# A spectral mixing kernel rewritten: row axis folded twice, products summed by matmul on 32x32 tiles, units of four PSUM banks

## The chip, the cores and the metric

The kernel runs on one core of a Trainium2 chip. The metric is the device time of one execution in microseconds. A profile of one execution shows each engine: PE (TensorE matmul; PEld its weight loads), DVE (VectorE), ACT (ScalarE), POOL (GpSimd) and SP, which here only issues transfers.

## The reference

Two inputs `A` and `B` each have spectral weights, both are applied to the same `x` (1 x 2048 x 1024, bf16), and a gate mixes the results:

```python
g = sigmoid((x * gate_w).sum(-1, keepdims=True))
X = rfft2(x.astype(float32))                 # over 2048 rows and 1024 columns
a = irfft2(X * (A_w_r + 1j * A_w_i)).astype(bfloat16)
b = irfft2(X * (B_w_r + 1j * B_w_i)).astype(bfloat16)
return g * a + (1 - g) * b
```

`w_r` and `w_i` are 2048 x 513. The transforms are computed as matmuls with constant cosine and sine matrices; the gate enters in the inverse row transform.

## The kernel before

The row index is split as s = 16 s2 + s1, with 128 values of s2 on the partitions and 16 of s1 along the free axis. The work goes through these steps:

- **f1** (L214 to L228): for each s1, eight matmuls (L218) of 256 columns transform along s2. The halves d and d + 512 are added and subtracted by the same matmuls (constants F and -F), so that frequencies along d fall into even and odd ones. A copy per s1, on ACT or DVE in turn (L226, L228), puts the result into `y`.
- **f2** (`f2`, L275): the transform along d, for one parity and a pair of row groups (a unit, n = 0 to 15: eight of even and then eight of odd columns): eight matmuls of 512 columns into a PSUM tile of two banks; ACT copies it to `T` (L279).
- **f3** (`f3`, L295, L303): the 16-point transform along s1 with twiddles, on 64x64 tiles of the array; for even columns also the extra column at the end of the spectrum, in a PSUM tile `pl` of its own, copied by DVE (L313). ACT copies the main part to `X` (L310).
- **cmul** (L325, L330, L331): on DVE, two products of X's real and imaginary part with the four weight matrices, then a subtraction and an addition that give the complex product `Y`.
- **i1** (L344): the inverse of f3, on 64x64 tiles, real and imaginary part apart; ACT copies each into `rl` (L349), and after the second POOL issues two DMAs (L354) that bring the rows into another order, into `Re` or `Ro`.
- **i2** (L367): the inverse transform along s2, with the gate multiplied into its constants (`EA`, `EB`), for a parity and two values of s1: 16 matmuls of 128 columns; ACT copies to `V` (L370).
- **i3** (L378): the inverse along d, eight matmuls of 512 columns. The even half is kept as fp32 (L384 on ACT, L386 on DVE); for the odd half DVE adds and subtracts (L389, L390), and SP stores the result (L391).
- **the gate**: `gate_hat` (L241) applies the gate's weights in the transformed domain, ACT copies (L245), a DMA from ACT's queue reshapes (L246), and `gate_z` (L254, L256) transforms back and takes the sigmoid. `gate_weights` (L261, L262) makes `EA` and `EB`.

The order of instructions on each engine is written out by hand in the loops from L394: unit n is in f2 while n - 1 is in f3 and cmul and n - 3 is in i1. `gate_hat` follows f2(0), and `gate_z` is issued at n = 2; the even half's i2 and i3 are woven into the last odd units; the rest of i2 and i3 follows alone. PSUM is used as three rotating tiles of two banks (`pp`) and one more tile. Engines work through their own queues in order; semaphores are set by the framework from the tiles that each instruction reads and writes.

Of the kernel before, what the change touches and what calls it, by code (L numbers as in the profile page):

```python
# [10 lines left out]
P = 128  # L11
S = 2048
D = 1024
NT = 16
NU = 8
# [5 lines left out]
WID = (257, 256)  # L21
PIT = (258, 256)
# [6 lines left out]
def quad_reps(t):  # L29
    return (0, 32, 16, 48) if t == 0 else (t, t + 32, t + 64, t + 96)  # L30


def half_k2(t, jh):
    a, b = quad_reps(t)[2 * jh:2 * jh + 2]
    if t == 0 and jh == 0:
        return (0, 64, 32, 96)
    return (a, 128 - a, b, 128 - b)


def half_rows(t, jh):  # L40
    return np.array([k2 + 128 * k1 for k2 in half_k2(t, jh) for k1 in range(16)])


def unit_rows(t):
    h = (0, 1) if t % 2 == 0 else (1, 0)
    return np.concatenate([half_rows(t, jh) for jh in h])


def make_constants():
    c = {}  # L50
    s2 = np.arange(128)
    F = np.zeros((128, NT, 2, 2, 2))
    E = np.zeros((NT, 2, 2, 2, 128))
    EZ = np.zeros((NT, 2, 2, 2, 128))
    for t in range(NT):
        for j, k2 in enumerate(quad_reps(t)):
            th = 2 * np.pi * s2 * k2 / 128
            F[:, t, j // 2, 0, j % 2] = np.cos(th)
            F[:, t, j // 2, 1, j % 2] = -np.sin(th)
            E[t, j // 2, 0, j % 2] = np.cos(th)  # L60
            E[t, j // 2, 1, j % 2] = np.sin(th)
            EZ[t, j // 2, 0, j % 2] = 2 * np.cos(th)
            EZ[t, j // 2, 1, j % 2] = -2 * np.sin(th)
            if k2 == 0:
                F[:, t, j // 2, 1, j % 2] = np.cos(np.pi * s2)
                E[t, j // 2, 1, j % 2] = np.cos(np.pi * s2)
                EZ[t, j // 2, 0, j % 2] = 1
                EZ[t, j // 2, 1, j % 2] = np.cos(np.pi * s2)
    F = F.reshape(128, 128)
    c["F1"] = _bf16np(np.concatenate([F, -F], axis=1))  # L70
    c["E"] = _bf16np(E.reshape(4, 4, 8, 128).transpose(0, 2, 1, 3).reshape(128, 128))
    c["EZ"] = _bf16np(EZ.reshape(128, 128) / 128)
    d1 = np.arange(512)
    i = np.arange(256)
    FD = np.zeros((512, 2, 2, 256))
    IG = np.zeros((2, 2, 256, 512))
    for eo in range(2):
        m = 2 * i + eo
        ph = 2 * np.pi * np.outer(d1, m) / D
        FD[:, eo, 0] = np.cos(ph)  # L80
        IG[eo, 0] = 2 * np.cos(ph).T
        if eo == 0:
            IG[0, 0, 0] = 1
        m = 2 * i + (2 if eo == 0 else 1)
        ph = 2 * np.pi * np.outer(d1, m) / D
        FD[:, eo, 1] = -np.sin(ph)
        IG[eo, 1] = -2 * np.sin(ph).T
        if eo == 0:
            FD[:, 0, 1, 255] = np.cos(np.pi * d1)
            IG[0, 1, 255] = np.cos(np.pi * d1)  # L90
    IG /= S * D
    c["FD"] = _bf16np(FD.reshape(4, 128, 2, 512).transpose(1, 2, 0, 3))
    c["IG"] = _bf16np(IG.reshape(2, 2, 2, 128, 512).transpose(3, 0, 1, 2, 4).reshape(128, 8, 512))
    s1 = np.arange(NS1)
    WF = np.zeros((128, NT, 3, 64))
    WI = np.zeros((128, NT, 3, 64))
    for t in range(NT):
        for jh in range(2):
            k = half_rows(t, jh)
            reps = quad_reps(t)[2 * jh:2 * jh + 2]  # L100
            al = np.zeros((NS1, 2, 2, 64), dtype=complex)
            be = np.zeros((2, 2, NS1, 64), dtype=complex)
            for p in range(64):
                w = np.exp(-2j * np.pi * k[p] * s1 / S)
                kk = k[p] % 128
                if kk in (0, 64):
                    cc = 0 if kk == 0 else 1
                    al[:, cc, 0, p] = w
                    be[cc, 0, :, p] = w.conj()
                    continue  # L110
                eps = 1 if kk in reps else -1
                j = reps.index(kk if eps > 0 else 128 - kk)
                al[:, 0, j, p] = w
                al[:, 1, j, p] = 1j * eps * w
                be[0, j, :, p] = w.conj()
                be[1, j, :, p] = 1j * eps * w.conj()
            al = al.reshape(64, 64)
            be = be.reshape(64, 64).T
            h = slice(64 * jh, 64 * jh + 64)
            WF[h, t, 0], WF[h, t, 1], WF[h, t, 2] = al.real, al.imag, -al.imag  # L120
            h = h if t % 2 == 0 else slice(64 - 64 * jh, 128 - 64 * jh)
            WI[h, t, 0], WI[h, t, 1], WI[h, t, 2] = be.real, be.imag, -be.imag
    c["WF"] = _bf16np(WF)
    c["WI"] = _bf16np(WI)
    return c
# [3 lines left out]
def gated_mix(ctx, tc, x_in, we_in, wo_in, gw_in, out):  # L129
# [5 lines left out]
    w_in = (we_in, wo_in)  # L135

    const = ctx.enter_context(tc.tile_pool(name="const", bufs=1))
    big = ctx.enter_context(tc.tile_pool(name="big", bufs=1))
    wp = ctx.enter_context(tc.tile_pool(name="wp", bufs=1))
    wk = ctx.enter_context(tc.tile_pool(name="wk", bufs=2))  # L140
    pp = ctx.enter_context(tc.tile_pool(name="pp", bufs=3, space=bass.MemoryType.PSUM))
    pl_pool = tc.alloc_tile_pool(name="plp", bufs=1, space=bass.MemoryType.PSUM)
# [4 lines left out]
    def ptile():  # L147
        return pp.tile([P, 1024], F32, name="pt", tag="pt")

    ctx.enter_context(tc.manual_schedule())  # L150
    warm = const.tile([P, 512], BF16, name="warm")
    nc.vector.memset(warm[:], 0.0)
    wps = ptile()
    for _ in range(6):
        nc.tensor.matmul(wps[:, 0:512], lhsT=warm[:, 0:128], rhs=warm[:], start=True, stop=True)  # L155
    F1 = const.tile([P, 2, 128], BF16, name="f1")
    nc.scalar.dma_start(F1[:].rearrange("p a b -> p (a b)"), dr["F1"])
    gws = const.tile([P, 8], BF16, name="gws")
    nc.scalar.dma_start(gws[:], gw_in)
    Re = big.tile([P, 16 * 1024], BF16, name="re")  # L160
    Ro = big.tile([P, 16 * 1024], BF16, name="ro")
    x = Re[:].rearrange("p (s d) -> p s d", s=NS1)
    for s0, n in ((0, 1), (1, 1), (2, 2), (4, 2), (6, 2), (8, 2), (10, 2), (12, 2), (14, 2)):
        nc.sync.dma_start(x[:, s0:s0 + n, :], xv[:, s0:s0 + n, :])
    FD = const.tile([P, 2, 4, 512], BF16, name="fd")
    WF = const.tile([P, NT, 3, 64], BF16, name="wf")
    WI = const.tile([P, NT, 3, 64], BF16, name="wi")
    IG = const.tile([P, 8, 512], BF16, name="ig")
    Ec = const.tile([P, 128], BF16, name="ec")
    Ez = const.tile([P, 128], BF16, name="ez")  # L170

    y = big.tile([P, 4, 2, 2 * NT, NS1, 4], BF16, name="y")
    Ws = {}
    wt = [wp.tile([P, 2064], BF16, name=f"w{k}", tag=f"w{k}") for k in range(4)]

    def load_w(n):
        par, u = n // NU, n % NU
        if n < 4 or 8 <= n < 12:
            w = wt[n % 4][:]
        elif n < 8:  # L180
            w = Ro[:, (n - 4) * 2064:(n - 3) * 2064]
        else:
            w = y[:, n - 12, 0].rearrange("p t s c -> p (t s c)")
        w = w[:, 0:8 * PIT[par]].rearrange("p (t a m) -> p t a m", t=2, a=4)
        nc.sync.dma_start(w, w_in[par][u])
        Ws[n] = w

    nc.sync.dma_start(FD[:, 0], dr["FD"][:, 0])
    nc.sync.dma_start(WF[:, 0:4], dr["WF"][:, 0:4])
    load_w(0)  # L190
    nc.sync.dma_start(Ez[:], dr["EZ"])
    nc.sync.dma_start(WI[:, 0:4], dr["WI"][:, 0:4])
    load_w(1)
    nc.sync.dma_start(WF[:, 4:16], dr["WF"][:, 4:16])
    load_w(2)
    nc.sync.dma_start(WI[:, 4:16], dr["WI"][:, 4:16])
    nc.sync.dma_start(Ec[:], dr["E"])
    for n in range(3, 8):
        load_w(n)
    nc.sync.dma_start(FD[:, 1], dr["FD"][:, 1])  # L200
    nc.sync.dma_start(IG[:], dr["IG"])

    gwz = const.tile([P, 8, 32], BF16, name="gwz")
    nc.gpsimd.memset(gwz[:], 0.0)
    gh = const.tile([P, 8], F32, name="gh")
    junk = const.tile([P, 8], F32, name="junk")
    nc.scalar.activation(junk[:], gwz[:, 0, 0:8], ACT.Sigmoid)
    nc.vector.tensor_scalar(gh[:], gws[:], 0.5, None, ALU.mult)
    gq = gwz[:].rearrange("p (q e) c -> p q e c", e=2)
    nc.vector.tensor_tensor(gq[:, :, 0, 0], gh[:, 0:4], gh[:, 4:8], ALU.add)  # L210
    nc.vector.tensor_tensor(gq[:, :, 1, 0], gh[:, 0:4], gh[:, 4:8], ALU.subtract)
# [54 lines left out]
    def hp(jh):  # L266
        return slice(64 * jh, 64 * jh + 64)
# [219 lines left out]
```

## Time and profile before

| | us |
|---|---|
| median of three runs | 145.82 (144.42 to 145.93) |
| profiled execution: its own time / its span | 144.42 / 144.4 |
| PE busy | 121.9 |
| DVE busy | 97.6 |
| ACT busy | 93.3 |
| POOL busy | 19.6 |

Matmuls count as busy from their start to a modelled end and overlap, so PE's busy time is not its work at full rate. Granted TensorE clock over the execution: 0.961 of full speed. Transfers: 29.19 MB in all, 20.55 MB from SP's queue and 8.41 MB from POOL's.

The page names a group of instructions by line, engine, operation, output and input. In a timeline a row has start, length, engine, line, operation, shapes and count; in square brackets stands what the engine waited for before it.

### The profile page before, as it was taken

To read this page: it belongs to the slowest core of one execution; us is meant where nothing else is said; L and a number is where in the kernel's file an instruction comes from. 1 tells how busy PE (TensorE), PEld (TensorE's weight loads), DVE (VectorE), ACT (ScalarE), POOL (GpSimd) and SP (SyncE) were. 2 spreads that over 40 slices of the span, in tenths; PEclk is the share of its full clock that TensorE was granted. 3 is DMA by queue.
4 is the path that set the end of the run, shared out by engine and by line. 5 is a ranking of instruction groups with operands and counts; after the bars stand their busy time and mean duration, and the time that the engine had idled before them with its cause. 6 is when DMAs were issued, how large, how long until landed. Compare 5 with 4: busy or idle time off the path is not lost.

```text
span 144.4 us, 2878 instructions
## 1 busy us (share of the span) xinstructions
PE 121.9 (84%) x1188; PEld 68.1 (47%) x1206; DVE 97.6 (68%) x113; ACT 93.3 (65%) x97; POOL 19.6 (14%) x37
## 2 busy tenths in 40 slices
PE   6999979929899898888867999868869999999910
PEld 2688844416344443334324345433455665756500
DVE  0177740089279999999999279599433456898990
ACT  4255546665699999999995899997935244253200
POOL 1000000000033222233333033033330000000000
PEclk9999999975799999999999999999999999999985
DMA  4999999968716999999865315527464000464553
GB/s 148 298 361 419 406 411 405 415 244 284 297 14 168 240 279 278 353 250 202 163 139 133 126 18 140 131 43 168 110 166 110 0 0 0 167 253 166 208 228 145
DMA packets 11088, 29.19 MB, mean 202 GB/s; under 512 B 3781, under 2 KB 4165, under 8 KB 10949
## 3 DMA queue, kind: packets, MB, share of 16 engines
q1 hardware_dynamic: 6048, 20.55, 38.3%
q0 software_dynamic: 4608, 8.41, 24.8%
q8 instruction: 9, 0.15, 0.5%
q10 hardware_dynamic: 420, 0.07, 0.3%
q14 instruction: 3, 0.02, 0.0%
HBM read 16.42 MB, written 4.19 MB: 143 GB/s over the span
## 4 chain that ended last, share of the span: by engine, by line
PE 55%; ACT 24%; DMA 9%; issue 4%; DVE 2%; another core or an unknown queue 2%; DVEq 1%; POOL 0%; ACTq 0%; POOLq 0%
PE pt L378 18%; PE pt L218 10%; PE pt L275 10%; ACT rl L349 10%; PE pv L367 9%; DMA re<-rl 5%; DMA zt<-zs 4%; ACT X L310 4%; ACT T L279 3%; PE pt L344 3%; ACT V L370 2%; PE pt L155 2%; ACT zs L245 2%; DVE ot L390 2%
## 5 line engine op out<-in xcount | busy, mean ns | idle before, releaser
L275 PE MATMUL pt<-fd,y 128*128 128x512 bf16 x117 | 30.5, 394 | 3.8 <-ACT rl L349 2.6
L349 ACT CAST rl<-pt 128x1024 bf16<-128x1024 f32 x32 | 32.9, 1038 | 0.0
L378 PE MATMUL pt<-ig,V 128*128 128x512 bf16 x121 | 29.6, 379 | 1.1 <-ACT V L370 0.7
L370 ACT CAST V<-pv 128x1024 bf16<-128x1024 f32 x16 | 16.3, 1021 | 19.2 <-PE pv L367 19.2
L344 PE MATMUL pt<-Y,wi 64*64 64x512 bf16 x256 | 20.1, 387 | 3.8 <-ACT T L279 0.8
L275 PEld LDWEIGHTS <-y 128*128 128x128 bf16 x128 | 12.6, 100 | 20.3 <-issue 8.6
L279 ACT CAST T<-pt 128x1024 bf16<-128x1024 f32 x16 | 16.3, 1017 | 8.3 <-PE pt L275 4.1
L378 PEld LDWEIGHTS <-V 128*128 128x128 bf16 x128 | 11.7, 98 | 13.9 <-ACT V L370 1.9
L354 POOL DMA_DIRECT2D re<-rl x16 | 9.6, 606 | 59.8 <-ACT rl L349 59.8
L310 ACT CAST X<-pt 128x1024 bf16<-128x1024 f32 x16 | 16.5, 1033 | 0.0
L218 PE MATMUL pt<-f_84,re 128*128 128x256 bf16 x128 | 15.6, 289 | 0.0
L218 PEld LDWEIGHTS <-re 128*128 128x128 bf16 x128 | 13.0, 103 | 3.1 <-DMA re<-in_x_dram 0.8
L228 ACT CAST y<-pt 128x1024 bf16<-128x1024 f32 x8 | 8.1, 1013 | 8.4 <-PE pt L218 8.4
L354 POOL DMA_DIRECT2D ro<-rl x16 | 9.5, 596 | 26.4 <-ACT rl L349 26.4
L386 DVE COPY re<-pt 128x1024 f32<-128x1024 f32 x5 | 6.1, 1225 | 10.2 <-PE pt L378 10.2
L226 DVE CAST y<-pt 128x1024 bf16<-128x1024 f32 x7 | 8.6, 1225 | 5.2 <-PE pt L218 5.2
L344 PEld LDWEIGHTS <-wi 64*64 64x64 bf16 x256 | 6.4, 106 | 11.9 <-issue 10.7
L389 DVE TENSOR_TENSOR ot<-pt,re 128x1024 bf16<-128x1024 f32 x8 | 9.8, 1224 | 3.0 <-PE pt L378 3.0
L367 PE MATMUL pv<-ea,re 128*128 128x128 bf16 x64 | 8.1, 219 | 2.9 <-DMA re<-rl 1.7
L295 PE MATMUL pt<-T,wf 64*64 64x512 bf16 (+2 forms) x192 | 9.8, 307 | 0.4 <-ACT T L279 0.3
L367 PEld LDWEIGHTS <-re 128*128 128x128 bf16 x128 | 7.5, 98 | 5.4 <-issue 2.5
L390 DVE TENSOR_TENSOR ot<-re,pt 128x1024 bf16<-128x1024 f32 x8 | 9.7, 1210 | 0.0
(96 smaller groups left out, 128.2 us busy)
## 6 DMA issues: line engine op xcount, KB each, us to landing
re<-rl POOLq DMA_DIRECT2D x16, 256.0 KB, 8.0
ro<-rl POOLq DMA_DIRECT2D x16, 256.0 KB, 5.1
out_dram<-ot SPq DMA_DIRECT2D x8, 512.0 KB, 2.6
re<-in_x_dram SPq DMA_DIRECT2D x7, 512.0 KB, 8.6
ro<-in_we_dram SPq DMA_DIRECT2D x4, 516.0 KB, 8.0
y<-in_wo_dram SPq DMA_DIRECT2D x4, 512.0 KB, 6.5
fd<-cst_fd SPq DMA_DIRECT2D x2, 512.0 KB, 9.1
ig<-cst_ig SPq DMA_DIRECT2D x1, 1024.0 KB
```

Of the source, the lines that this page charges most:

```text
L218: nc.tensor.matmul(ps[:, q * 256:(q + 1) * 256], lhsT=x[:, s1, h * 512 + q * 128:h * 512 + (q + 1) * 128], rhs=(bc(F1[:, 0, :]).to_broadca ...
L275: nc.tensor.matmul(ps[:, tt * 512:(tt + 1) * 512], lhsT=y[:, q, par, 2 * t:2 * t + 2, :, :].rearrange("p j s c -> p (j s c)"), rhs=FD[:, p ...
L279: nc.scalar.copy(out=T[:].rearrange("p a b -> p (a b)"), in_=ps[:])
L295: nc.tensor.matmul(ps[ho, tt * 512 + dst:tt * 512 + dst + ln], lhsT=WF[hp(jh), 2 * u + tt, w, :], rhs=T[hp(jh), tt, src:src + ln], start=( ...
L310: nc.scalar.copy(out=xo, in_=ps[:].rearrange("p (t r m) -> p t r m", t=2, r=2))
L344: nc.tensor.matmul(ps[hp(jh), tt * 512:(tt + 1) * 512], lhsT=WI[hin, 2 * u + tt, w, :], rhs=Y[hin, k, 2 * tt:2 * tt + 2, o:o + 256], start ...
L349: nc.scalar.copy(out=rl[:, :, r, :], in_=ps[:].rearrange("p (t m) -> p t m", t=2))
L354: nc.gpsimd.dma_start(RR[par][p0:p0 + 29:4, :, :], rl[:, tt].rearrange("p r m -> p (r m)"))
L367: nc.tensor.matmul(ps[:, s * 512 + ch * 128:s * 512 + ch * 128 + 128], lhsT=RR[par][:, s1, c0 + 256 * ab:c0 + 256 * ab + 128], rhs=Ew[:, s ...
L370: nc.scalar.copy(out=V[:].rearrange("p s c k -> p (s c k)"), in_=ps[:])
L378: nc.tensor.matmul(ps[:, s * 512:(s + 1) * 512], lhsT=V[:, s, ch, :], rhs=IG[:, par * 4 + ch, :], start=(ch == 0), stop=(ch == 3))
L390: nc.vector.tensor_tensor(ot[:, :, 1, :], ev, pv, ALU.subtract)
```

## The change

The kernel is rewritten; what is computed stays. The parts:

- **Second fold along d.** Input columns are permuted on the host into the order i, 511 - i, 512 + i, 1023 - i (i = 0 to 255), and the output is permuted back. On the chip `fold` adds and subtracts the halves d and d + 512 with DVE or POOL instructions (for the first s1 `f1u` does it in the matmuls as before), and f1's matmuls add and subtract the mirrored quarters. f2 then contracts 256 values of d in place of 512 for each of cosine and sine.
- **i3 folded likewise.** It makes the cosine and the sine part for 256 values of d apart; `ce` copies both to bf16, `pm` adds and subtracts them (two instructions of 512 elements, DVE or POOL) and `fin` combines the even and the odd half (two of 1024).
- **32x32 tiles.** f3 and i1 work on groups of four row frequencies, 32 partitions by 32, sixteen tiles of the array at a time, over four PSUM banks.
- **No sums on DVE.** `prod` leaves the two products as they are; i1 takes their four terms in four accumulating matmuls per tile, in place of two on `Y`.
- **Units of four banks** (8 units in place of 16), with one PSUM tile of eight banks addressed by bank; copies span one to four banks and are shared between ACT and DVE by a list.
- **Odd columns first**: units 0 and 1 are odd, 2 to 5 mixed, 6 and 7 even; i2 and i3 run over the odd half and then over the even half.
- **The last column of the even spectrum** is computed for all units at once (`pre1`, `pre2`, matmuls of one column) and copied into place by POOL (`xn`).
- **Order**: one list, `ORDER`, gives the sequence of all steps with PSUM bank and engine.

```diff
+UNITS = [[(4 * h + b, 1) for b in range(4)] for h in range(2)]
+UNITS += [[(2 * u, 0), (2 * u, 1), (2 * u + 1, 0), (2 * u + 1, 1)] for u in range(4, 8)]
+UNITS += [[(4 * h + b, 0) for b in range(4)] for h in range(2)]
...
+    def fold(s0, n, eng):
+        e = nc.vector if eng == "d" else nc.gpsimd
+        for k, op in enumerate((ALU.add, ALU.subtract)):
+            e.tensor_tensor(xf[:, s0:s0 + n, 512 * k:512 * k + 512], x[:, s0:s0 + n, 0:512], x[:, s0:s0 + n, 512:1024], op)
...
+    def f1(s1, g0):
+        for uv in range(2):
+            for blk in range(2):
+                for h in range(2):
+                    c0 = uv * 512 + h * 256 + blk * 128
+                    nc.tensor.matmul(PS[:, g0 + uv, blk * 256:blk * 256 + 256], lhsT=xf[:, s1, c0:c0 + 128],
+                                     rhs=fn if h else ff, start=(h == 0), stop=(h == 1))
...
+    def f2(u, g0):
+        for b, (t, par) in enumerate(UNITS[u]):
+            for cs in range(2):
+                for blk in range(2):
+                    nc.tensor.matmul(PS[:, g0 + b, 256 * cs:256 * cs + 256],
+                                     lhsT=y[:, par, blk, KK[par, cs], 4 * t:4 * t + 4].rearrange("p q s c -> p (q s c)"),
+                                     rhs=FD[:, par, cs, blk, :], start=(blk == 0), stop=(blk == 1))
...
+    def f3(u, g0):
+        for k, (w, src, dst, ln) in enumerate(((0, 0, 0, 512), (2, 256, 0, 256), (1, 0, 256, 256))):
+            for b, (t, par) in enumerate(UNITS[u]):
+                for a in range(4):
+                    qo = 32 * ((a + b) % 4)
+                    nc.tensor.matmul(PS[qo:qo + 32, g0 + b, dst:dst + ln], lhsT=WF[32 * a:32 * a + 32, t, w, :],
+                                     rhs=T[0][32 * a:32 * a + 32, b, src:src + ln], start=(k == 0), stop=(k == 2))
...
+    def prod(u, s, r, b0, nb):
+        M = 257 if any(par == 0 for t, par in UNITS[u]) else 256
+        xb = X[u % 2][:, b0:b0 + nb, r, 0:M].rearrange("p b (a m) -> p b a m", a=1).to_broadcast([P, nb, 4, M])
+        nc.vector.tensor_tensor(pr[u % 2][r][:, b0:b0 + nb, :, 0:M], xb, W[s][:, b0:b0 + nb, :, 0:M], ALU.mult)
+
+    def i1(u, r, g0):
+        terms = ((0, 0, (0, 2)), (1, 1, (1, 3)), (0, 1, (3, 0)), (1, 0, (3, 0)))
+        for k, (xr, wr, ws) in enumerate(terms):
+            for b, (t, par) in enumerate(UNITS[u]):
+                o = 1 if par == 0 and r == 1 else 0
+                for a in range(4):
+                    q = 32 * ((a + b) % 4)
+                    rhs = pr[u % 2][xr][q:q + 32, b].rearrange("p (h w) m -> p h w m", w=2)[:, :, wr, o:o + 256]
+                    nc.tensor.matmul(PS[32 * a:32 * a + 32, g0 + b, :], lhsT=WI[q:q + 32, int(t == 0 and a == 0), ws[r], :],
+                                     rhs=rhs, start=(k == 0), stop=(k == 3))
...
+    def i3(par, v, g0):
+        vt = V[seq.index((par, v)) % 3]
+        for s in range(2):
+            for r in range(2):
+                for blk in range(2):
+                    nc.tensor.matmul(PS[:, g0 + s, 256 * r:256 * r + 256], lhsT=vt[:, s, 256 * r + 128 * blk:256 * r + 128 * blk + 128],
+                                     rhs=IG[:, 4 * par + 2 * r + blk, :], start=(blk == 0), stop=(blk == 1))
+
+    def ce(par, v, g0, b0, nb, eng):
+        copy(eng, CS[seq.index((par, v)) % 3][:, b0:b0 + nb, :], PS[:, g0 + b0:g0 + b0 + nb, :])
+
+    def pm(par, v, k, eng):
+        e = nc.vector if eng == "d" else nc.gpsimd
+        cs = CS[seq.index((par, v)) % 3].rearrange("p s (r m) -> p s r m", r=2)
+        e.tensor_tensor(EO[par][v % len(EO[par])][:, k], cs[:, :, 0], cs[:, :, 1], (ALU.add, ALU.subtract)[k])
+
+    def fin(v, k, eng):
+        e = nc.vector if eng == "d" else nc.gpsimd
+        a, b = (EO[par][v % len(EO[par])][:] for par in range(2))
+        e.tensor_tensor(OT[v % 3][:, :, k].rearrange("p s e m -> p e s m"), a, b, (ALU.add, ALU.subtract)[k])
...
+    for name, *a in order:
+        ops[name](*a)
...
+ORDER = [
...
+    ("ye", 12, 4, 0, 2, "d"), ("f1", 10, 0), ("ye", 10, 0, 0, 1, "a"), ("ye", 10, 0, 1, 1, "d"), ("f2", 0, 0), ("te", 0, 0, 2, 2, "d"),
+    ("te", 0, 0, 0, 2, "a"), ("f2", 1, 4), ("f3", 0, 0), ("xe", 0, 0, 0, 2, "a"), ("te", 1, 4, 0, 1, "d"), ("xe", 0, 0, 2, 2, "d"),
+    ("te", 1, 4, 1, 3, "a"), ("gh", 4), ("zse", 4), ("prod", 0, 0, 0, 0, 4), ("f3", 1, 0), ("pre1", 5), ("xe", 1, 0, 3, 1, "d"),
...
+    ("pm", 0, 5, 1, "d"), ("fin", 5, 1, "d"), ("pm", 0, 6, 0, "d"), ("pm", 0, 6, 1, "d"), ("st", 3), ("ce", 0, 7, 0, 0, 2, "a"), ("fin", 5, 0, "p"),
...
+]
```

In the list `te`, `xe`, `re` and `ve` are the copies out of PSUM after f2, f3, i1 and i2, `ye` that after f1, `ex` the exchange DMA that POOL issues, `gh`, `zse`, `gz`, `sig` and `gw` the gate's steps, `ld` a load and `st` a store. The engine is the letter at the end: a for ACT, d for DVE, p for POOL. Arrays are laid out anew: FD, IG, WF and WI are smaller, and the inverse constants E now hold the twiddles for all 16 values of s1.

More of the change, by code (lines that the diff above doesn't have):

```diff
@@ L14 @@
 NT = 16
-NU = 8
 NS1 = 16
@@ L51, in make_constants @@
     s2 = np.arange(128)
[L52 to L68, printed above, removed]
+    s1 = np.arange(NS1)
@@ new lines, in gated_mix, with sb @@
+    ctx.enter_context(tc.manual_schedule())
+    def sb(name, shape, dt=BF16):
+        return const.tile([P] + list(shape), dt, name=name)
+    PS = pp.tile([P, 8, 512], F32, name="ps")
+    warm = sb("warm", [512])
+    nc.vector.memset(warm[:], 0.0)
+    for _ in range(6):
+        nc.tensor.matmul(PS[:, 7, :], lhsT=warm[:, 0:128], rhs=warm[:], start=True, stop=True)
+    F1 = sb("f1", [3, 128])
+    gws = sb("gws", [8])
+    nc.scalar.dma_start(F1[:], dr["F1"].rearrange("p (a b) -> p a b", a=3))
@@ L203, in gated_mix @@
[L203 to L211, printed above, removed]
```

595 lines of the change are left out of this document (244 added, 351 removed), and 50 rows, old and new, of the table ORDER.

## The prediction

> **What bounds the kernel now.** I read the busy totals first, then the busy time by stage, then the chain of work that ended last.
>
> ```profile
> PE 121.9 (84%) x1188; PEld 68.1 (47%) x1206; DVE 97.6 (68%) x113; ACT 93.3 (65%) x97; POOL 19.6 (14%) x37
> ...
> PE 55%; ACT 24%; DMA 9%; issue 4%; DVE 2%; another core or an unknown queue 2%; DVEq 1%; POOL 0%; ACTq 0%; POOLq 0%
> ```
>
> No engine fills the span, so the stages differ. In the table by stretch the columns are length, then busy us of PE, weight load, DVE, ACT, POOL:
>
> ```profile
> 1.20:20.10 18.90, 18.23 (x134) 13.71 (x134) 8.99 (x10) 10.08 (x11) 0.00 (x0) 1.00 0.97 356
> 20.10:37.50 17.40, 13.79 (x121) 6.87 (x128) 8.32 (x11) 9.06 (x8) 0.00 (x0) 0.81 0.90 347
> 37.50:76.50 39.00, 32.96 (x395) 15.10 (x400) 34.73 (x44) 37.17 (x40) 10.81 (x18) 1.00 0.82 211
> 97.20:136.10 38.90, 36.48 (x338) 22.53 (x341) 25.57 (x26) 18.78 (x20) 3.55 (x6) 1.00 0.38 120
> ```
>
> The reader is to see: PE sets the column transform (to 20.1) and the closing i2/i3 stage (97.2 to 136.1, 36.5 of 38.9). From 37.5 to 76.5 ACT, 37.2 of 39.0, is the bound, DVE close behind. Between 20.1 and 37.5 nothing is full; the chain in order of time says why, the gate's round trip:
>
> ```profile
> 23.94 2.35 ACT zs L245
> ...
> 26.32 5.80 DMA zt<-zs
> ```
>
> Prices come from start-to-start distances of neighbours in the timeline, since an instruction's recorded time overlaps the next one's:
>
> ```profile
> 29.60 1.24 DVE L325 TENSOR_TENSOR p_383<-X,w_106 128x2056 bf16<-128x2056 bf16 x1
> 30.75 1.23 DVE L325 TENSOR_TENSOR p_385<-X,w_106 128x2056 bf16<-128x2056 bf16 x1
> 32.02 0.70 DVE L330 TENSOR_TENSOR Y<-p_383,p_385 128x1028 bf16<-128x1028 bf16 x1
> 32.63 0.69 DVE L331 TENSOR_TENSOR Y<-p_383,p_385 128x1028 bf16<-128x1028 bf16 x1
> ...
> 47.28 1.04 ACT L310 CAST X<-pt 128x1024 bf16<-128x1024 f32 x1
> 48.18 1.04 ACT L349 CAST rl<-pt 128x1024 bf16<-128x1024 f32 x1
> ...
> 130.86 1.22 DVE L389 TENSOR_TENSOR ot<-pt,re 128x1024 bf16<-128x1024 f32 x1 [0.27 <-PE pt L378]
> 132.00 1.21 DVE L390 TENSOR_TENSOR ot<-re,pt 128x1024 bf16<-128x1024 f32 x1
> ```
>
> DVE takes 1.15 us for 2056 and 0.61 for 1028 bf16 elements (0.08 + n/1920) and 1.14 for 1024 read from PSUM (0.08 + n/960). ACT takes 0.91 for 1024 (0.06 + n/1200).
>
> **The change, part by part.**
>
> *PE loses.* f2 keeps 128 matmuls but streams 256 columns, not 512. Eight of 512 take 1.73 us (113.21 to 114.94 in the closing stage: 0.216 each), so 27.7 us become 128 x 0.109 = 14.0. i3 falls in the same way, from 27.7 to 14.0. i2 stays at 256 x 0.0556 = 14.2. f1 has 136 matmuls of 256 columns for 128: +0.9.
>
> *i1 and f3 on 32x32 tiles* are 1024 and 384 matmuls, with 128 of one column more (pre2). The nearest rows are the 64x64 ones:
>
> ```profile
> 53.22 0.63 PE L344 MATMUL pt<-Y,wi 64*64 64x512 bf16 x8
> 53.67 0.60 PE L295 MATMUL pt<-T,wf 64*64 64x512 bf16 x12
> 54.11 0.21 PE L303 MATMUL pl<-T,wf 64*64 64x1 bf16 x8
> ```
>
> Eight 512-column matmuls occupy 0.45 us until the next group starts: four tiles run side by side, 0.22 a round. Eight of one column take 0.21 in all, of which one alone is 0.167 (mean of that group): eight starts fit into 0.04. So I take a round of sixteen as one pass, 0.22: i1 is 64 rounds, 13.9 us, against 20.1 busy now for half as many terms; f3 is 3.5 against 6.9. Bounds: 13.5 ns a pair from below, and from above the 55.6 ns at which the 128-column pairs of i2 follow each other for whole groups, the shortest spacing that the trace shows sustained. I take the lower end, because the one-column row is of the same kind.
>
> [...]
>
> *DVE and ACT.* The adds L330/L331 go (32 x 0.61 = 19.7 us of DVE); i1 sums their terms. The products remain: 24 instructions, 36.1 us. Evacuation of f1, f2, f3 and i1 keeps its volume (16 + 64 blocks of 1024). New on DVE are 24 fold instructions, 8.8 us. The closing stage now evacuates i3 as bf16 (ce) and rebuilds with pm (32 of 512) and fin (16 of 1024), instead of L384/L386/L389/L390. Adding the list of the new kernel by these prices:
>
> - until the first f2: PE 16, DVE 13.5, ACT 11.1;
> - until the first i2: DVE 52.5, ACT 47.3, PE 36;
> - from there: PE 29.1, DVE 27.6, ACT 23.6, POOL 14 instructions and 8 exchanges.
>
> So **DVE becomes the bound of the middle**, by a small margin, and the end is balanced between PE and DVE.
>
> *POOL arithmetic* has no row. The nearest are DVE's 0.42 us for 512 elements and POOL's own memset L204, 0.311 for 256 with one pass (0.098 for one element): 0.83 ns an element a pass. One pass gives 0.52, three passes (two reads, a write) 1.37 for 512. I take two passes, 0.95, and 1.8 for 1024: in the closing stage 11 x 0.95 + 3 x 1.8 + 8 exchanges x 0.6 = 20.7 of some 33 us. It fits; at three passes 27.8, just.
>
> *The gate* is issued behind unit 1 and used some 15 us later; its 5.8 us of DMA lie beside products, so the PE hole (28.9 to 32.2) goes. If that cover fails, DVE is late by those 3 us.
>
> *Transfers* fall from 29.2 MB by half of FD and IG and most of WF and WI, about 2 MB. Queued behind the same 4.2 MB of x at 400 GB/s, FD, WF and the first weights (2 MB) land near 19, before their first use near 27. Exchanges stay 8.4 MB in 24 issues for 32. Odd columns are complete after unit 5, so i2 of them needs no transfer of units 6 and 7.
>
> **The sum**, against this execution's own 144.4 us (span and time agree; the median of the three runs is 145.8, 1% more).
>
> 1. First f2: now 20.15. PE 1.4 more, then a last half-bank copy of 0.6: **21.5**.
> 2. Fill: f2 twice (3.5), f3 (0.6), xe (0.9): first product at **27.0**; DVE has 2.9 us of its work done by then.
> 3. The other 49.6 us of DVE at the 92% that ACT reaches now in its stage (four copies, 3.66, in a period of 3.96): 53.9, to **81**. ACT (47.3) and PE (36 and some 6 of tile-mode changes, 0.1 to 0.2 each) lie beside it.
> 4. Closing: 1.5 to start, eight odd pairs at PE's 1.77 and i1's rest (15), eight even ones by DVE, 14.7 plus waits (17): 33.5, to **114.5**, against 38.9 now.
> 5. Tail: last ce, pm, two fin (2.9), then the store to the end, 3.7 as now (140.7 to 144.4): **121**, or **122** on the level of the median.
>
> **Rivals.**
>
> *Packed tiles are issued no faster than other matmuls (slower than before).* Place: i1 and f3 in the middle. Their price p per pair makes PE there 22 + 1536p plus 3 of fill. It decides above (83 - 25)/1536 = 38 ns, where the middle has eaten the gain of 23. At i2's 55.6 ns the middle is 110 and the whole 172. For it: no row sustains more than 28 pairs in 0.93 us (33 ns), and 16 kB of instructions for PE must be fetched about twice as often. Against it: the one-column burst, and that those 28 pairs were held by the array. 12%. A milder form, 30 ns, gives about 132.
>
> *POOL and DVE get into each other's way.* POOL now reads two SBUF operands, which it never does before. If each such instruction keeps DVE's two-operand ones waiting, the closing stage's 15.8 us of POOL arithmetic fall on DVE for the 15.2 of its 27.6 us that are of that kind: 15.8 x 0.55 = +8.7, **131**. [...] With it I count the in-order queues: one T buffer, exchange buffers freed only on landing (5 to 8 us), 80% instead of 92% in steps 3 and 4, +11, **133**. Together 25%.
>
> *Everything fits*: DVE without gaps and POOL at DVE's speed, 113. 9%.
>
> **Chances.** Forecast (116 to 126) 48%; collisions and stalls (126 to 137) 25%; better 9%; between 137 and 144, 3%; within 1%, which is what a measurement tells from no change, 3%; slower 12%. Range 112 to 140.
>
> **What would show it.** DVE the busiest engine in the middle, near 90%; PE busy about 80 to 95 in all; groups of sixteen i1 matmuls about 0.22 us apart; the gate's DMA ending no wait of PE; POOL's 512-element instructions near 1 us with no DVE gap beside them. Wrong if i1's rounds take over 0.5 us, if DVE idles over 10 us in the middle, or if its two-operand instructions lengthen beside POOL's.

## The result, and the profile after

The changed kernel takes **156.09 us** (median; 153.84 to 159.56), the kernel before 145.88 (144.42 to 147.36) beside it: 1.064 of it, with a 95% interval of 1.049 to 1.078. Some executions of a kernel take a few per cent longer than its fastest, and the ratio leaves them out. It is slower; the forecast was 122. The profiled execution took 155.48 us with a span of 153.0, and all that follows is read against that span.

The busy totals of the changed kernel, and from the same page the granted clock of TensorE in 40 slices and the row of instruction packets of queue q8 (packets, MB, share):

```profile
span 153.0 us, 5049 instructions
...
PE 103.9 (68%) x2270; PEld 78.3 (51%) x2270; DVE 115.6 (76%) x128; ACT 86.7 (57%) x83; POOL 49.3 (32%) x55
...
PEclk9999789999577899999877899956999999997555
...
q8 instruction: 17, 0.28, 0.7%
```

PE has indeed become shorter (121.9 before), and ACT too. DVE grew by 18 us, POOL by 30, and now no engine is near its span. TensorE's clock drops again and again in the middle, where before it fell once ahead of the last slices; and queue q8 has 17 packets of instructions, 16 kB each, where the page of before has 9 of that size:

```profile
PEclk9999999975799999999999999999999999999985
...
q8 instruction: 9, 0.15, 0.5%
```

The table by stretch of the changed kernel, cut at the ends of the prediction's steps (first f2, first product, first i2, last i3, end; columns as before: length, then busy us of PE, weight load, DVE, ACT, POOL, the granted clock, the DMA share, GB/s):

```profile
1.20:26.57 25.37, 20.58 (x142) 15.08 (x143) 18.18 (x35) 13.30 (x16) 4.66 (x2) 0.93 0.89 335
26.57:32.89 6.32, 5.57 (x104) 4.30 (x108) 3.05 (x4) 2.94 (x3) 0.00 (x0) 1.00 0.01 3
32.89:103.54 70.65, 46.52 (x1585) 30.59 (x1577) 54.12 (x39) 45.38 (x36) 20.97 (x28) 0.85 0.66 189
103.54:136.12 32.58, 31.23 (x463) 28.36 (x448) 27.15 (x34) 23.07 (x27) 17.10 (x16) 0.97 0.30 83
136.12:153.00 16.88, 0.00 (x0) 0.00 (x0) 12.84 (x17) 2.02 (x2) 5.94 (x3) 0.61 0.46 186
```

| step | forecast, us | after, us | difference |
|---|---|---|---|
| 1 to the first f2 | 21.5 | 26.57 | +5.1 |
| 2 to the first product | 5.5 | 6.32 | +0.8 |
| 3 middle, to the first i2 | 54 | 70.65 | +16.6 |
| 4 closing, to the last i3 | 33.5 | 32.58 | -0.9 |
| 5 tail | 6.5 | 16.88 | +10.4 |
| span | 121 | 153.0 | +32.0 |

The whole miss lies in three rows. In the middle DVE is busy for 54.1 of 70.65 us, 77% where 92% was forecast, and PE for 46.5, so neither is full: both wait. Of step 3's 16.6 us, 4.5 are work of DVE (54.1 instead of 49.6) and some 12 its idle time (16.5 instead of 4.3). DVE's products wait for i1 there (4.7 of the 5.1 us ahead of them, in the groups); and PE, by the view of waits (engine and line, what it waited for, us in total, times, longest), for nothing that the profile shows:

```profile
PEld L308 <- issue: 18.9, 19, 3.9
...
PE ps L308 <- issue: 7.9, 3, 2.9
...
PEld L247 <- issue: 7.0, 7, 3.7
```

L308 is i1, L247 f2. In the timeline of the changed kernel such a stop lies inside one i1 step, eight matmuls after its start; beside it, DVE and POOL:

```profile
90.94 0.41 PE L308 MATMUL ps<-p,wi 32*32 32x512 bf16 x8
...
92.09 7.85 DVE L297 TENSOR_TENSOR p<-x,w 128x2056 bf16<-128x2056 bf16 x3
92.50 2.13 POOL L346 TENSOR_TENSOR late<-late,e 128x1024 bf16<-128x1024 bf16 x1
94.10 1.96 PE L308 MATMUL ps<-p,wi 32*32 32x512 bf16 x120 [2.75 <-issue]
...
94.70 3.00 POOL L348 TENSOR_TENSOR e<-e,late 128x1024 bf16<-128x1024 bf16 x1
```

Two things are seen at once. Three products that take 1.23 us each elsewhere take 7.85 together while POOL works on two SBUF operands. And PE stands from 91 to 94.1. Counting PE's instructions in the order of their start (weight loads included), the long stops of this kind all stand at numbers 193 + 256k, and each ends some 2.4 us after a packet on the instruction queue has started. Worked out from the trace:

```
number  last start  next start  stop   packet starts  from packet to next start
1217    47.41       48.16       0.75   45.75          2.41
1729    58.15       59.12       0.97   56.66          2.46
2241    67.28       69.04       1.76   66.55          2.49
2497    72.32       74.96       2.64   72.36          2.61
2753    78.46       81.71       3.25   79.40          2.31
3009    86.88       87.36       0.48   84.78          2.58
3265    90.96       94.10       3.14   91.69          2.41
3521    97.68      101.67       3.99   99.31          2.35
```

Their sum is 17.0 us. In four rows (1729, 2241, 3265, 3521) PE's next matmul also waited for a copy or a product, which ended 0.4, 0.8, 1.2 and 3.4 us into the stop; so some 11 of the 17 us are stops that nothing else explains, and the sums of stops below hold such waits too. Two more gaps at such places, 0.8 us at 449 and 1.4 us at 961, end with a copy and are not counted. In the trace of before, counted in the same way, there is no such stop: its blocks of 256 last 12 to 16 us, those here, in the middle, 1.8 to 7.6 with the stops.

So three theories to tell apart, besides the price of the packed tiles: **L**, POOL's two-operand work holds up DVE's ("the lock" below); **F**, PE uses up its instructions faster than they come; **G**, the gate, since one PE gap of 3.7 us follows ACT's copy of zs and its issue of zt. The timeline of the changed kernel (ACTq is ACT's own queue):

```profile
33.67 2.51 ACT L194 CAST zs<-ps 128x512 bf16<-128x512 f32 x1 [0.36 <-PE ps L326]
...
36.22 1.10 ACTq L332 DMA_DIRECT2D zt<-zs  x1
37.42 1.44 ACT L194 CAST x<-ps 128x1536 bf16<-128x1536 f32 x1 [1.23 <-DMA zt<-zs]
...
38.91 0.37 PE L247 MATMUL ps<-fd,y 128*128 128x256 bf16 x1 [3.65 <-ACT x L194]
```

### The profile page after: what moved, and what is told of

Its sections match the earlier page's. It is cut to its first block, busy times and chain, and to the rows that moved or that the text cites. A ratio compares the mean times of both kernels' runs of the same rounds, so it can differ in the third digit from the quotient of the medians.

```text
span 153.0 us, 5049 instructions
## 1 busy us (share of the span) xinstructions
PE 103.9 (68%) x2270; PEld 78.3 (51%) x2270; DVE 115.6 (76%) x128; ACT 86.7 (57%) x83; POOL 49.3 (32%) x55
## 5 line engine op out<-in xcount | busy, mean ns | idle before, releaser
L297 DVE TENSOR_TENSOR p<-x,w 128x2056 bf16<-128x2056 bf16 (+3 forms) x24 | 41.4, 1764 | 5.1 <-PE ps L308 4.7
L194 ACT CAST rl<-ps 128x2048 bf16<-128x2048 f32 (+2 forms) x16 | 24.0, 1522 | 15.7 <-PE ps L308 13.1
L308 PE MATMUL ps<-p,wi 32*32 32x512 bf16 x1024 | 23.0, 438 | 14.2 <-issue 7.9
L308 PEld LDWEIGHTS <-wi 32*32 32x32 bf16 x1024 | 13.8, 90 | 21.5 <-issue 18.9
L247 PE MATMUL ps<-fd,y 128*128 128x256 bf16 x128 | 18.8, 311 | 6.3 <-ACT x L194 5.1
L194 ACT CAST w<-ps 128x1024 bf16<-128x1024 f32 (+1 forms) x19 | 16.4, 887 | 7.5 <-PE ps L358 4.9
L247 PEld LDWEIGHTS <-y 128*128 128x128 bf16 x128 | 13.7, 110 | 11.2 <-issue 7.0
L228 PE MATMUL ps<-f,r 128*128 128x256 bf16 x120 | 15.0, 288 | 3.5 <-DVE r L217 3.5
L358 PE MATMUL ps<-late,r 128*128 128x128 bf16 x128 | 16.8, 227 | 0.3 <-DVE late L194 0.3
L369 PE MATMUL ps<-ig,w 128*128 128x256 bf16 x128 | 16.3, 273 | 1.0 <-ACT w L194 1.0
L358 PEld LDWEIGHTS <-r 128*128 128x128 bf16 x256 | 16.3, 102 | 1.3 <-issue 1.1
L358 PE MATMUL ps<-e,r 128*128 128x128 bf16 x128 | 16.7, 227 | 0.0
L228 PEld LDWEIGHTS <-r 128*128 128x128 bf16 x120 | 12.2, 104 | 6.1 <-DVE r L217 4.0
L217 DVE TENSOR_TENSOR r<-r 128x512 bf16<-128x512 bf16 (+1 forms) x24 | 12.8, 597 | 1.2 <-DMA r<-in_x_dram 1.1
```

The costliest lines, as they stand in the source:

```text
L194: (nc.scalar.copy if eng == "a" else nc.vector.tensor_copy)(out=out, in_=in_)
L217: e.tensor_tensor(xf[:, s0:s0 + n, 512 * k:512 * k + 512], x[:, s0:s0 + n, 0:512], x[:, s0:s0 + n, 512:1024], op)
L228: nc.tensor.matmul(PS[:, g0 + uv, blk * 256:blk * 256 + 256], lhsT=xf[:, s1, c0:c0 + 128], rhs=fn if h else ff, start=(h == 0), stop=(h == 1))
L247: nc.tensor.matmul(PS[:, g0 + b, 256 * cs:256 * cs + 256], lhsT=y[:, par, blk, KK[par, cs], 4 * t:4 * t + 4].rearrange("p q s c -> p (q s ...
L297: nc.vector.tensor_tensor(pr[u % 2][r][:, b0:b0 + nb, :, 0:M], xb, W[s][:, b0:b0 + nb, :, 0:M], ALU.mult)
L308: nc.tensor.matmul(PS[32 * a:32 * a + 32, g0 + b, :], lhsT=WI[q:q + 32, int(t == 0 and a == 0), ws[r], :], rhs=rhs, start=(k == 0), stop=( ...
```

## The experiments

Times are medians, except where one execution is named; each ratio stands against the kernel before on the same chip (145.5 to 147.9). All edits but one start from the changed kernel.

### POOL's arithmetic to DVE

```diff
-    ("fold", 10, 2, "p"),
+    ("fold", 10, 2, "d"),
...
-    ("gw", 0, 8, 0, "p"),
+    ("gw", 0, 8, 0, "d"),
...
-    ("pm", 1, 3, 1, "p"),
+    ("pm", 1, 3, 1, "d"),
...
```

(17 steps of the list: one fold, two gw, eleven pm, three fin.)

> All 17 arithmetic steps of POOL (fold, gw, pm, fin) are given to DVE in the same places of the list; POOL keeps xn and the exchange DMAs. Theory L (a POOL instruction that reads two operands and a DVE instruction that reads two operands keep each other waiting): the 14.6 us by which DVE's two-operand instructions exceed their undisturbed times go, DVE gets 8.1 us of new work; first f2 from 26.6 to about 23, closing stage from 45.6 to about 39, total from 153 to about 145 (141 to 148). Rival (POOL's help is worth what it costs, the list is simply longer than thought): DVE has 8 us more and the total rises by 2 to 5 us.

147.32 us, 1.001 (0.993 to 1.010): as theory L said, some 9 us less than the change as it came, though DVE has 18 instructions more. The groups by form of the changed kernel:

```profile
L378 DVE TENSOR_TENSOR p<-w 128x512 bf16<-128x512 bf16 x6 | 8.2, 1399 | 0.1
...
L217 DVE TENSOR_TENSOR r<-r 128x1024 bf16<-128x1024 bf16 x2 | 5.1, 2598 | 0.0
...
L378 POOL TENSOR_TENSOR y<-late 128x512 bf16<-128x512 bf16 x6 | 7.3, 1229 | 6.9 <-ACT late L194 5.0 <-DVE late L194 1.8
```

and of this one:

```profile
L217 DVE TENSOR_TENSOR r<-r 128x1024 bf16<-128x1024 bf16 x4 | 2.5, 684 | 0.0
...
L378 DVE TENSOR_TENSOR p<-w 128x512 bf16<-128x512 bf16 x6 | 2.3, 420 | 0.1
```

A 512-element sum on DVE takes 0.42 us alone and 1.40 beside POOL; a 1024-element fold 0.68 and 2.60. Over the changed kernel DVE's two-operand instructions take 18.9 us more than the same forms undisturbed (3.8 in the fold, 4.3 in three products, 7.6 in pm, 3.2 in fin; the 14.6 of the expectation leave out the products). Here the excess is nil, and DVE's total falls from 115.6 to 104.3. The first f2 now starts at 21.64 (forecast 21.5), so all of step 1's miss was the fold on POOL. By its table, middle and tail:

```profile
27.95:100.91 72.96, 48.05 (x1584) 30.63 (x1576) 51.09 (x41) 45.75 (x36) 16.45 (x26) 0.81 0.66 184
...
135.02:146.40 11.38, 0.00 (x0) 0.00 (x0) 7.18 (x15) 1.01 (x1) 0.00 (x0) 0.61 0.57 231
```

The tail is 11.4 instead of 16.9, and step 4 1.5 longer (34.1), so steps 4 and 5 together are 4.0 us shorter. The middle is no shorter, and its stops at 193 + 256k sum to 20.0 us: theory F is another matter.

### i1 and f3 on 64x64 tiles

```diff
-                for a in range(4):
-                    q = 32 * ((a + b) % 4)
-                    rhs = pr[u % 2][xr][q:q + 32, b].rearrange("p (h w) m -> p h w m", w=2)[:, :, wr, o:o + 256]
-                    nc.tensor.matmul(PS[32 * a:32 * a + 32, g0 + b, :], lhsT=WI[q:q + 32, int(t == 0 and a == 0), ws[r], :],
+                for a in range(0, 4, 2):
+                    q = zpart(a, b)
+                    rhs = pr[u % 2][xr][q:q + 64, b].rearrange("p (h w) m -> p h w m", w=2)[:, :, wr, o:o + 256]
+                    nc.tensor.matmul(PS[32 * a:32 * a + 64, g0 + b, :], lhsT=WI[q:q + 64, int(t == 0 and a == 0), ws[r], :],
```

WI and WF hold each pair of 32x32 blocks on the diagonal of a 64x64 one; f3 and pre2 change alike.

> f3, i1 and the one-column step on 64x64 tiles with block-diagonal constants: half as many matmuls and weight loads (about 1,540 PE instructions fewer), twice the array time (i1 27.7 us for 13.9, f3 7 for 3.5); all else as in the changed kernel. Theory F (PE waits for its instructions at every 256th one when a block of 256 has been used up in less time than the next takes to arrive): some 6 such places fewer in the middle, and those left are covered by 1.7 us of queued work; standstills of 16 to 18 us fall below 8, total about 146 (142 to 151) although the array works 17 us longer. Rival S (the middle is held by the order of the list and by waits for copies, or by the array): total rises by 3 to 12 us, to 156 to 165.

156.18 us, 1.061 (1.051 to 1.070). By the time that is the rival's 156, and F's 146 is missed; by the trace the stops at 193 + 256k are gone, every one, as F said. In their place stand the array's extra 17 us (by the price of a round; PE's busy time is 9.5 us longer) and a new wait of 6.2 us: unit 5's copies wait for unit 3's exchange.

### i1's matmuls in halves

```diff
-                    nc.tensor.matmul(PS[32 * a:32 * a + 32, g0 + b, :], lhsT=WI[q:q + 32, int(t == 0 and a == 0), ws[r], :],
-                                     rhs=rhs, start=(k == 0), stop=(k == 3))
+                    for h in ((slice(0, 2),) if k == 0 else (slice(0, 1), slice(1, 2))):
+                        nc.tensor.matmul(PS[32 * a:32 * a + 32, g0 + b, 256 * h.start:256 * h.stop],
+                                         lhsT=WI[q:q + 32, int(t == 0 and a == 0), ws[r], :], rhs=rhs[:, h], start=(k == 0), stop=(k == 3 and h.stop == 2))
```

> i1's second to fourth term in matmuls of 256 columns instead of 512: the same columns through the array, 768 more matmuls and as many weight loads (1,536 instructions, 6 blocks of 256). Theory F: six more standstills of 2 to 3.5 us, total 165 to 175. Rival S: the array time is the same, so the total stays within 2 us of 153.

185.88 us in one execution, span 183.6: more than F's 175, far from 153. The stops sum to 38.3 us (the longest 7.8), and the granted clock stood at half for 48 us up to the last matmul, against 27 in the changed kernel.

### Shift the numbering

```diff
+    for i in range(32):
+        r0, c0 = 32 * (i // 4 % 4), 32 * (i % 4)
+        nc.tensor.matmul(PS[c0:c0 + 32, 3 + i // 4 % 4, 0:1], lhsT=warm[r0:r0 + 32, 0:32], rhs=warm[r0:r0 + 32, 0:1], start=True, stop=True)
```

(In the warm-up, before any data.)

> 32 matmuls of one column are added to the warm-up before the input arrives: every later PE instruction stands 64 places further on, nothing else changes. Theory F: the standstills stay at places 193 + 256k of the PE's instructions and so come before other matmuls, 32 matmuls earlier in the list (in i1 of unit 3 before its 25th rather than its 57th matmul); total 149 to 157. Rival S (the standstills belong to these steps, by their semaphores): they stay before the same matmuls, total within 1 us of 153.

162.29 us in one execution, above both forecasts by 5. The stops stayed at 193 + 256k, and so moved by 64 instructions to other steps: those above 0.4 us sum to 19.9, the longest 4.62 (at 78 us) and 6.10 (at 99). So they belong to the count and not to any step or its data. Why the time rose by 6 isn't shown; the clock was at half for 44 us up to the last matmul.

### The gate's transfer on SP's queue

```diff
-        nc.scalar.dma_start(zt[:], zs[0:97:32].rearrange("p q c s -> p (q c s)"))
+        nc.sync.dma_start(zt[:], zs[0:97:32].rearrange("p q c s -> p (q c s)"))
```

(On the kernel of the first experiment.)

> The kernel of e1_pool_to_dve, with the gate's transfer zt issued from SP's queue instead of ACT's. Theory G (ACT stands 3.7 us behind the gate's copy and the issue of its transfer, and with it xe of unit 1 and f2 of unit 2, where PE's gap is 3.8 us): the issue leaves ACT, the gap shrinks by 1 to 1.5 us and the time falls from 147.3 to 145 to 146.5. Rival, that the middle is paced by PE's instruction supply anyway: the gap shrinks but the stops at every 256th PE instruction absorb it, 147 to 148.

145.11 us (141.1 to 148.0), 0.996 by the medians. PE's gap shrinks from 3.8 to 2.4, as theory G said; whether the time follows can't be told in this scatter. The stops sum to 17.3.

### No POOL arithmetic, zt on SP, and 64x64 tiles

(The edits of three experiments above, together.)

> The kernel of e5_zt_sp with f3, i1 and pre2 on 64x64 tiles as in e2_tiles64 (half as many PE instructions of these steps, twice the array time, some 17 us more). If the losses add (lock 9, gate 1 to 2, instruction supply replaced by array time): 144 to 147. If the exchange between units decides (in e2_tiles64 the copies of unit 5 waited 6.2 us for unit 3's exchange to land): 148 to 152 with a wait of ACT or DVE for that transfer of over 4 us. No stop of over 0.5 us at any 256th PE instruction in either case.

**141.42 us, 0.969 (0.959 to 0.979)**: below both kernels, and below the sum that was expected. No stop at 193 + 256k over 0.14 us. Against the kernel of the experiment before, on 32x32 tiles, that is 3.7 us less by the medians and 1.1 by the fastest execution of each: with the other losses out of the way, the halved count of instructions makes up for its 17 us of array time. What is late next stands in its view of waits and in the timeline:

```profile
ACT rl L207 <- DMA r<-rl: 6.9, 2, 6.3
```

```profile
81.47 2.78 ACT L207 CAST rl<-ps 128x2048 bf16<-128x2048 f32 x2 [6.29 <-DMA r<-rl]
83.39 1.07 PE L273 MATMUL ps<-t,wf 64*64 64x512 bf16 x8 [6.23 <-ACT rl L207]
```

There are two rl buffers, and unit 3's exchange, issued at 67.1 and 69.1, lands 12 us later; the DMA engines are busy for eight to nine tenths or more of every slice from 55 to 81 us.

### No weights for units 3 to 7

```diff
-    ("ld", "w", 3, 0),
...
-    ("ld", "w", 4, 1),
...
-    ("ld", "w", 6, 0), ("ld", "w", 5, 2),
...
-    ("ld", "w", 7, 1),
```

(On the kernel of the first experiment. Left out: five loads; these units multiply by other units' weights.)

> The kernel of e1_pool_to_dve without the loads of the weights of units 3 to 7 (these units multiply by what units 0 to 2 left there; 5.3 MB less to transfer, every instruction of PE, DVE, ACT and POOL as before). If the instruction packets come late because they queue behind the weights' transfers: the stops at every 256th PE instruction fall from 20 us to under 8, and the time from 147.3 to 133 to 139. If an instruction packet takes its time whatever else is moved: stops of 14 to 24 us, time 143 to 148.

139.79 us (137.9 to 146.7), 0.952 (0.941 to 0.962), between the two forecasts. The profiled execution was the slowest of these, 146.65 us, so it can't show where the others gained; in it the stops sum to 19.6, as before. So in this execution the packets come no sooner without the weights' transfers; for the faster ones that isn't shown. That 5.3 MB less is worth some 7 us would fit the exchange's wait above, which no trace of a faster execution confirms.

### The kernel before, with as many PE instructions

```diff
+        for i in range(32):
+            c, tt = i % 4, i // 4 % 2
+            z = 32 * ((c + tt) % 4)
+            nc.tensor.matmul(ps[32 * c:32 * c + 32, tt * 512:tt * 512 + 1], lhsT=WI[z:z + 32, 2 * u, 0, 0:32], rhs=Y[z:z + 32, 0, 0, 0:1], start=True, stop=True)
```

> The kernel before with 32 one-column matmuls on 32x32 tiles ahead of each i1 step (1024 pairs, so that PE has about as many instructions as the changed kernel; columns that i1 overwrites, no other work). By the packed rounds of the changed kernel 32 of them occupy the array about 0.1 us, 3 to 4 us in all, beside an ACT that bounds that stage. Theory F (PE waits for instructions): blocks of 256 instructions that last 11 to 15 us in the middle are used up in 5 to 7, stops of 1 to 4 us appear at every 256th, time 152 to 166. Rival (the stops of the changed kernel belong to its data or its order): no such stops, 146 to 150.

152.85 us, 1.049 by the medians, inside F's range. In its view of waits PE is idle twice, for nothing that the profile shows, once in f3 (L295) and once in i1 (L349):

```profile
PE pt L295 <- issue: 2.6, 1, 2.6
...
PE pt L349 <- issue: 1.5, 1, 1.5
```

This trace has 2,230 weight loads and 2,206 matmuls, so 24 matmuls have no record, and a plain count of the rows runs behind. Counted with the matmul that belongs to each weight load, three stops stand at 193 + 256k: 2.83 us at 1473, 0.57 at 1729 and 1.89 at 1985 (from start to start; the first and the last are the two lines above). They end 2.6 to 2.8 us after their packet has started, and no copy or product ends them. So more PE instructions, on the old data in the old order, are enough to bring stops: the rival falls. But F had them at every 256th instruction, and the ten other places between 705 and 3777 pass without one. PE has 5.4 us of work in a block there on average; the three that end in a stop hold 4.0 to 5.9, and blocks of 4.0 to 4.7 pass as well, with the next packet started within 1.6 us of the block's beginning. The packets of the stops started 3.3 to 4.8 us after it. How the 7 us divide between the stops (5.3) and the groups themselves, which hold PE for some 0.2 us each, isn't separated.

### E and IG loaded at the start

```diff
-    ("ld", "w", 2, 2), ("f1u", 0, 0),
+    ("ld", "w", 2, 2), ("ld", "E"), ("ld", "IG"), ("f1u", 0, 0),
...
-    ("prod", 6, 0, 1, 0, 4), ("ld", "E"), ("i1", 5, 1, 4),
+    ("prod", 6, 0, 1, 0, 4), ("i1", 5, 1, 4),
...
-    ("xn", 7, "p"), ("ld", "IG"), ("re", 5, 0, 0, 0, 2, "a"),
+    ("xn", 7, "p"), ("re", 5, 0, 0, 0, 2, "a"),
```

(On the kernel with these three edits.)

> The kernel of e6_sp_tiles64 with the loads of E and IG (1 MB) issued behind the first three units' weights, at the start, instead of between units 5 and 6. Theory X (in e6_sp_tiles64 the DMA engines are 99% busy from 57 to 81 us, so unit 3's exchange lands 12 us after its issue and unit 5's copies wait for it; PE's gap there is 6.6 us): 1 MB less at some 300 GB/s is 3.3 us, the gap falls to 3 to 4.5 us and the time from 141.4 to 137.5 to 140. Rival (the exchange is slow by itself, by its many small packets): gap and time as they were, 140.5 to 142.

**138.40 us (137.9 to 139.1), 0.938 (0.931 to 0.945)**, the best of all. The exchange's wait is the one that shrank, by its view of waits, and i1's waits for nothing that the profile shows last 1.3 us at most:

```profile
PEld L322 <- issue: 7.3, 20, 1.3
...
ACT rl L207 <- DMA r<-rl: 3.6, 2, 3.4
```

Its table by stretch, from the first product on:

```profile
28.02:91.87 63.85, 54.04 (x873) 34.30 (x865) 50.65 (x41) 45.84 (x36) 16.00 (x25) 0.95 0.70 187
91.87:123.69 31.82, 31.13 (x420) 27.36 (x416) 27.41 (x51) 23.85 (x28) 3.48 (x6) 1.00 0.38 111
123.69:135.00 11.31, 0.00 (x1) 0.00 (x0) 7.17 (x15) 1.01 (x1) 0.00 (x0) 0.59 0.57 233
```

### Four copies from DVE to ACT in the closing stage

```diff
-    ("ce", 1, 0, 4, 0, 2, "d"),
+    ("ce", 1, 0, 4, 0, 2, "a"),
...
-    ("ce", 1, 1, 2, 0, 2, "d"),
+    ("ce", 1, 1, 2, 0, 2, "a"),
...
-    ("ce", 1, 6, 6, 0, 2, "d"),
+    ("ce", 1, 6, 6, 0, 2, "a"),
...
-    ("ve", 0, 1, 6, 0, 2, "d"),
+    ("ve", 0, 1, 6, 0, 2, "a"),
```

> The kernel of e8_early_e_ig with four two-bank copies of the closing stage moved from DVE to ACT (4.6 us off DVE, 3.6 onto ACT). If DVE's backlog of pm and fin sets the end (in e1_pool_to_dve DVE works 7.3 us beyond the last i3): 2 to 4 us less than e8_early_e_ig. Rival, that PE with ACT's copies sets the stage and the backlog is only shifted: within 1 us of it, or 1 to 2 us more.

138.52 us, 0.939 (0.931 to 0.947): no difference, the rival's time. DVE is busy 23.1 us in the stage instead of 27.4, and the tail is 11.0 instead of 11.3. But the backlog does set the end: in both kernels DVE works without a gap from its last wait (at 114 and 115 us) to its last fin, on the same 35 instructions. The four copies stood ahead of that wait, at 97 to 111 us, and without them DVE waits longer there, at last 1.8 us for PE's i3.

### f3 alone back on 32x32 tiles

```diff
-                for a in range(0, 4, 2):
-                    qo = zpart(a, b)
-                    nc.tensor.matmul(PS[qo:qo + 64, g0 + b, dst:dst + ln], lhsT=WFs[t // 8][32 * a:32 * a + 64, t % 8, w, :],
+                for a in range(4):
+                    qo = zpart(a, b)
+                    nc.tensor.matmul(PS[qo:qo + 32, g0 + b, dst:dst + ln],
+                                     lhsT=WFs[t // 8][32 * a:32 * a + 32, t % 8, w, 32 * (a % 2):32 * (a % 2) + 32],
```

(In f3 of the kernel of the experiment before.)

> The kernel of e9_closing with f3 alone back on 32x32 tiles (384 matmuls instead of 192, 3.5 us less array time; i1 stays on 64x64). Theory F: a unit has 256 PE instructions in some 7 us; blocks of 256 last about 7 us, which the supply just bears: stops of under 3 us in all, time 0 to 2.5 us less than e9_closing. Rival (any step on 32x32 tiles with long rows brings the stops back): stops of 5 us or more, time 1 to 4 us more.

142.46 us (138.3 to 144.5), 0.963 by the medians. One stop of the kind is left, 0.4 us, as F said (another gap at such a place, 1.3 us, ends with the gate's sigmoid), but no time is won. Unclear.

### All but the tiles

(No new line: the kernel with E and IG loaded early, on the changed kernel's 32x32 tiles.)

> The kernel of e8_early_e_ig with f3, i1 and pre2 back on the changed kernel's 32x32 tiles: 17 us less of array time, 1536 PE instructions more. If the stops at every 256th PE instruction cost what e5_zt_sp showed (17.3 us, with the clock's half speed behind them): 142 to 146, ratio to the kernel before 0.965 to 0.99, so 4 to 7 us worse than on 64x64 tiles. Rival (the stops mattered only beside the full transfer queues, which the early loads relieve): stops under 6 us and 130 to 136.

144.11 us (139.4 to 145.5), 0.990 by the medians, with stops of 16.4 us. On 64x64 tiles it was 138.40 (137.9 to 139.1) and 0.938; by the fastest executions alone, each against the fastest of the kernel before, 0.973 stands against 0.940. So the packed tiles lose against 17 us more array time, by 3 to 5%, and the relieved transfers don't stop the stops.

## Why the prediction was wrong, step by step

Three terms failed: step 3's 92% of DVE (77% measured, with PE in its stops at 193 + 256k, 17.0 us in all, and DVE standing behind PE), step 1 without the lock between POOL and DVE, and step 5's 2.9 us of DVE's work behind the last i3 (12.8 measured, 7.2 without POOL).

**Packed tiles: the term was right, what feeds them was left out.** The changed kernel's table for i1 alone, in one stretch (length, PE, weight load):

```profile
44.44:45.20 0.76, 0.76 (x64) 0.54 (x43) 1.00 0.00 0
```

Rounds of sixteen lie some 0.22 us apart, 13.6 ns a pair: close to the lower end, which I had taken, and sustained. The sixteen starts of a round on different tiles fit into 0.03 to 0.13 us. The rival said that packed tiles are *issued* no faster. They are, outside the stops. "16 kB of instructions for PE must be fetched about twice as often" stood in it as an argument and got no price. The stops fit it: they stand 256 instructions apart, and each ends 2.3 to 2.6 us after a packet of 16 kB has started. But the rival's sum does not give this time: 17.0 us over 1,536 pairs are 11 ns a pair on top of 13.6, and its formula makes 63 us of that for steps 2 and 3 together, where 77.0 were measured and PE was not full. The changed kernel's trace has 17 packets, 0.28 MB, for 4,540 instructions of PE, and that of before 9, 0.15 MB, for 2,394: one to some 266 in both. Before, blocks of 256 that last 12 to 16 us pass without a stop; the stops here stand behind blocks of 1.0 to 5.3 us of work.

**Step 1, +5.1, and step 5: the lock, right in kind, wrongly placed, and right in size by luck.** The rival "POOL and DVE get into each other's way" gave +8.7; the first experiment measured 9. It was an estimate on an "if" that no row of before showed. Measured here: DVE's 0.42 us become 1.40 and 0.68 become 2.60 beside POOL. I had put all of it into the closing stage. There, steps 4 and 5 together, it cost 4.0 us (49.5 against 45.5); the other 5 lie at the fold in step 1, which the rival didn't count. So 8.7 and 9 agree by luck. POOL's own durations, 1.15 to 1.33 us for 512 and 2.1 to 3.0 for 1024, are nearer to three passes (1.37) than to the two that I took.

**Step 2** held, at +0.8.

**Step 3, +16.6: the 92%.** DVE's work was right (49.6 forecast; 51.1 in the first experiment, with 1.4 us of gw taken from POOL); in the changed kernel the lock adds 4.3 us to it. Its share was borrowed from ACT, in a stage with no short blocks and no shared buffer. With the stops gone (best kernel) it is 50.65 of 63.85, or 79%, about the 80% of the rival of in-order queues, but with PE busy for 54 us of it on 64x64 tiles. What holds DVE there (one T buffer, two rl buffers whose exchange lands late, PE) wasn't separated. With the stops in, it is 77% in the changed kernel and 70% in the first experiment. No run has 32x32 tiles without stops, so how much of the 12 us of idle time is theirs stays open. That products cover the gate's DMA was right for the transfer and wrong for its issue: ACT, which issues it, stood behind the zs copy, 2.5 us, and the issue, 1.2, and PE's gap is 3.7 us.

**Step 4** held, at 32.6 against 33.5; 31.8 in the best kernel.

**Step 5, +10.4: the backlog.** I counted 2.9 us of DVE's work behind the last i3. The list puts eight fin and six pm there: 7.2 us even without POOL, and the tail then takes 11.4. Steps 4 and 5 together were to be 40.0; they are 49.5, and 43.1 in the best kernel.

**PE busy 80 to 95**: 103.9. In steps 2 and 3 it is 52.1 instead of 36, with a granted clock of 0.85 in the middle; each stretch at half clock there starts inside or just behind a gap of PE.

**The cases were taken for exclusive.** Each rival stood against the forecast by itself. But nothing in them excluded the others: 121 + 8.7 (lock) + 11 (queues) is 141, without anything new. The stops' 17 on top would give 158, close to 156 by luck: stops and queues share the same idle time of DVE, 12 us more than forecast, and the tail's backlog is in neither. The range ended at 140 because at most one was to happen.

## What to carry to other kernels

When many short matmuls run side by side, count PE's instructions by stage as well as its array time: behind blocks of 256 (weight loads counted) with some 3.5 us of work PE stood still here for 2.6 to 4.0 us each, and tiles of twice the edge with half the instructions were 3 to 5% faster in spite of an estimated 17 us more array time (by 0.22 us a round). Before you count, see that each weight load has its matmul in the trace. Keep two-operand SBUF work off POOL while DVE does the same kind: a sum of 0.42 us on DVE took 1.40 beside it here, and handing 17 such steps back to a busier DVE won 9 us. And when rivals don't exclude one another, add them up before the range is set.

## What the runs showed of the hardware that was not expected

- **Stops at places 256 PE instructions apart.** PE goes on 2.3 to 2.6 us after the packet has started in the changed kernel, and 2.6 to 2.8 in the kernel before with as many instructions. In the changed kernel the packets of the stops from 1729 on start 3.1 to 5.2 us after the block before was entered; at the three places from 1473 to 3777 that pass without one (1473, 1985 and 3777) it is 1.1, 1.2 and 2.2 us. What sets that start is open: the stops stay without the weights' transfers (19.6 us) and with the early loads (16.4), and in the kernel before, with as many instructions, ten of thirteen places between 705 and 3777 pass without one.
- **A slower clock behind PE's gaps.** TensorE's granted clock falls to half for 3.4 us at a time, or a multiple of that: 27 us in the changed kernel before the tail, against 6.8 before. Behind the stops at 2497, 2753 and 3521 (2.6 to 4.0 us) it fell, behind the 3.1 us at 3265 it did not. How much of the time that costs wasn't separated.
- **A late exchange.** With the stops gone, the same 512 KB exchange that lands within some 8 us otherwise took 12 behind full DMA engines; moving 1 MB of constants ahead took 3 us off that wait, and the ratio fell from 0.969 to 0.938.
